# Row-tiled matmuls of 32 rows by 128 outputs issued as four of 32 by 32 in a cross network

## The chip, the cores and the metric

The kernel runs on one NeuronCore of a Trainium2 chip. The metric is the device time of one execution in microseconds (us); lower is better. The engines named below are TensorE (PE: matmuls; its weight loads are listed apart as PEld), VectorE (DVE), ScalarE (ACT), GpSimd (POOL) and SyncE (SP, which here issues most of the DMAs).

## The reference

A six-layer cross network (DCN v2) over a batch of 4096 rows with 416 features, all in bfloat16:

```python
B, F, D, L = 4096, 26, 16, 6
Din = min(F * D, 1024)          # 416
x0: (B, Din)   ws: (L, Din, Din)   bs: (L, Din)

def reference(x0, ws, bs):
    x = x0
    for l in range(ws.shape[0]):
        x = x0 * (x @ ws[l] + bs[l]) + x
    return x
```

## The kernel before

**Layout.** Through the first five layers the activations are held transposed: features on the 128 partitions, batch along the free dimension. 416 features are three full blocks of 128 (`XM`, indexed by k on the input side and m on the output side) and a remainder of 32. The batch is two halves (`s`) of 2048, and each half is four groups (`g`) of 512 columns. The remainder would fill only 32 partitions, so the remainders of the four groups are stacked: `XR` holds group g's 32 features on partitions 32g to 32g+31. The weight rows that belong to the remainder (`WR`) stand four times in SBUF, once on each of these strips, so that each group finds its weights on its own partitions.

**TensorE as tiles.** A matmul here has a tile position (row, column) in the 128 by 128 array, in steps of 32. Its rows are the partitions of the two inputs, its columns the partitions of the PSUM output. Matmuls at different positions can stand in the array at the same time. Three helpers issue the matmuls of layers two to five:

- `mm_full` (L181): for one output block m and one group g, the three k blocks, each as four matmuls of 128 rows and 32 outputs at the column positions 0, 32, 64, 96. The four write the four partition quarters of one PSUM bank.
- `mm_row` (L187): the share of the remainder in output block m, for all four groups at once: four matmuls of 32 rows and 128 outputs at the row positions 0, 32, 64, 96. Group g writes the whole of its own bank, `pts[g // 2][:, g % 2, :]`. This is the function that is changed.
- `mm_rem` (L193 and L198): the 32 outputs of the remainder, for all four groups, as matmuls of 128 rows and 32 outputs.

**PSUM.** Each output block of one half takes two PSUM tiles of two banks (`new_pts`); the pool holds four such tiles, which is all eight banks.

**Elementwise.** `ew_main` (L165, L166, L169) takes a PSUM tile of 128 by 1024: ScalarE adds the bias and writes bfloat16 to SBUF, VectorE multiplies by x0 and adds the old x. `ew_rem` (L173 to L175) does the same for the remainder.

**Order.** Layers two to five (l = 1 to 4) take the six pairs of half and output block two at a time, ta and tb. TensorE's order in one such step is: `mm_full` of ta for the four groups (48 matmuls), `mm_row` of ta, which closes ta's sums, `mm_row` of tb, which opens tb's sums, then `mm_full` of tb (48 matmuls), which closes them. So two `mm_row` calls stand next to each other, and a layer has three such row blocks, twelve over the four layers. After the first step of a layer `mm_rem` runs for both halves. The order in the program is the order on the engine; the tile framework puts semaphore waits where a buffer or an input demands it.

The first layer (`first_layer`: L214 full products of 128 by 128, L221 row products) and the last layer (L327, L333, L336: the activations become the stationary side so that rows of the batch come out on the partitions) have helpers of their own.

Of the kernel before, what the change touches and what calls it, by code (L numbers as in the profile page):

```python
# [16 lines left out]
def kernel(  # L17
# [7 lines left out]
    nc = tc.nc  # L25
# [7 lines left out]
    NG = 4  # L33
    CW = 512
# [18 lines left out]
    WR = const.tile([P, L, D], BF16)  # L53
# [129 lines left out]
                                 tile_position=(0, 32 * q))  # L183

    def mm_row(l, s, m, pts, curR, first, last):
        for g in range(NG):
            nc.tensor.matmul(pts[g // 2][:, g % 2, :], lhsT=WR[32 * g:32 * g + 32, l, 128 * m:128 * m + 128],  # L187
                             rhs=curR[32 * g:32 * g + 32, CW * s:CW * s + CW],
                             start=first, stop=last, tile_position=(32 * g, 0))

    def mm_rem(l, s, pr, cur, curR):
        for g in range(NG):
# [88 lines left out]
    cur, curR = XM[1], XR[1]  # L281
    for l in range(1, LL):
# [3 lines left out]
        pts = {}  # L286
# [8 lines left out]
        for n in range(0, len(tiles), 2):  # L295
            ta, tb = tiles[n], tiles[n + 1]
            pts[ta] = new_pts()
            for g in range(NG):
                mm_full(l, ta[0], ta[1], g, pts[ta], cur, True, False)
            mm_row(l, ta[0], ta[1], pts[ta], curR, False, True)  # L300
            pts[tb] = new_pts()
            mm_row(l, tb[0], tb[1], pts[tb], curR, True, False)
            if feeds_last and n == 4:
                xl_rem(0)
            finish(ta)
            for g in range(NG):
                mm_full(l, tb[0], tb[1], g, pts[tb], cur, False, True)
            finish(tb)
            if n == 0:
                rem_pair(l, cur, curR, nxtR, feeds_last)  # L310
        if feeds_last:
            xl_rem(1)
        cur, curR = nxt, nxtR

    l = LL
# [97 lines left out]
```

## Time and profile before

| what | before |
|---|---|
| time, median of 3 runs | 131.17 us (130.72 to 131.19) |
| span of the profiled execution, first to last instruction | 128.9 us |
| median less that span, what lies around it | 2.3 us |
| TensorE matmuls busy | 123.1 us, 96% of the span |
| VectorE busy | 107.1 us, 83% |
| ScalarE busy | 86.9 us, 67% |
| granted TensorE clock, mean | 0.998 of full speed |
| one layer of layers three to five (46.2 to 65.4, 65.4 to 84.6, 84.6 to 103.8 us) | 19.2 us each |
| L187, matmuls of 32 by 128 with 512 columns | 96, mean 379 ns each |
| L181, matmuls of 128 by 32 with 512 columns | 1152, mean 379 ns each |

How to read it: matmuls are pipelined and several stand in the array at once, so their lengths overlap and must not be added up; the end of a matmul is modelled. What counts is when the next one starts. In the views, `32*128 32x512 bf16 x8` means eight matmuls on 32 rows and 128 columns of the array that each stream 32 partitions by 512 elements. In the chain of work that ended last, each line is a start, a length, and the work that filled it. "idle before <-releaser" is the time in which the engine stood before the instruction, and what ended it; "issue" means that nothing in the profile explains the wait.

### The profile page before, as it was taken

To read this page: it belongs to the slowest core of one execution; us is meant where nothing else is said; L and a number is where in the kernel's file an instruction comes from. 1 tells how busy PE (TensorE), PEld (TensorE's weight loads), DVE (VectorE), ACT (ScalarE), POOL (GpSimd) and SP (SyncE) were. 2 spreads that over 40 slices of the span, in tenths; PEclk is the share of its full clock that TensorE was granted. 3 is DMA by queue.
4 is the path that set the end of the run, shared out by engine and by line. 5 is a ranking of instruction groups with operands and counts; after the bars stand their busy time and mean duration, and the time that the engine had idled before them with its cause. 6 is when DMAs were issued, how large, how long until landed. Compare 5 with 4: busy or idle time off the path is not lost.

```text
span 128.9 us, 3973 instructions
## 1 busy us (share of the span) xinstructions
PE 123.1 (96%) x1690; PEld 54.9 (43%) x1690; DVE 107.1 (83%) x197; ACT 86.9 (67%) x99; POOL 5.9 (5%) x18
## 2 busy tenths in 40 slices
PE   6999999999999999999999999999999999999960
PEld 2343443354444444444444444444444445445420
DVE  1032979999999898989898989898989899898991
ACT  0426783987848577848668848668847896569670
POOL 4022200600000000000000000000000000000000
PEclk9999999999999999999999999999999999999999
DMA  3999999999990000000000000000297999995754
GB/s 106 237 203 217 170 158 260 247 328 333 336 299 11 5 0 8 0 0 5 0 5 0 5 0 5 0 5 0 42 166 164 123 219 178 187 323 188 231 179 139
DMA packets 42102, 16.37 MB, mean 127 GB/s; under 512 B 30906, under 2 KB 42084, under 8 KB 42084
## 3 DMA queue, kind: packets, MB, share of 16 engines
q1 hardware_dynamic: 39416, 15.56, 54.6%
q10 hardware_dynamic: 2668, 0.56, 2.3%
q8 instruction: 13, 0.21, 0.7%
q14 instruction: 5, 0.04, 0.1%
HBM read 6.15 MB, written 3.41 MB: 74 GB/s over the span
## 4 chain that ended last, share of the span: by engine, by line
PE 80%; DMA 8%; DVE 5%; issue 2%; SPq 1%; ACT 1%; DVEq 0%
PE pt L181 49%; PE ph L214 9%; DMA XM<-in_x_dram 8%; PE py L327 8%; PE pt L187 5%; PE pr L198 5%; DVE t L355 3%; DVE o L344 2%; PE pr L193 2%; SPq L76 1%; PE py L333 1%; PE ph L221 1%; PE py L336 1%; ACT t L354 1%; PE pr L157 0%
## 5 line engine op out<-in xcount | busy, mean ns | idle before, releaser
L181 PE MATMUL pt<-XM,WM 128*32 128x512 bf16 x1152 | 65.2, 379 | 0.0
L165 ACT ACTIVATE t<-pt,bM 128x1024 bf16<-128x1024 f32 x48 | 49.6, 1115 | 18.3 <-PE pt L187 18.3
L166 DVE TENSOR_TENSOR t<-t,XM 128x1024 bf16<-128x1024 bf16 x60 | 41.4, 690 | 5.3 <-ACT t L165 5.3
L169 DVE TENSOR_TENSOR XM<-t,XM 128x1024 bf16<-128x1024 bf16 x60 | 41.8, 696 | 3.4
L181 PEld LDWEIGHTS <-WM 128*32 128x32 bf16 x1152 | 29.7, 97 | 33.8 <-issue 5.1
L354 ACT CAST t<-py 128x416 bf16<-128x416 f32 (+1 forms) x23 | 14.8, 642 | 4.8 <-PE py L327 2.1
L327 PE MATMUL py<-WM,XM 128*128 128x416 bf16 x96 | 17.7, 340 | 0.0
L214 PE MATMUL ph<-XM,WM 128*128 128x512 bf16 x72 | 16.5, 379 | 0.1
L165 ACT ACTIVATE t<-ph,bM 128x1024 bf16<-128x1024 f32 x12 | 12.5, 1114 | 4.4 <-PE ph L221 4.4
L327 PEld LDWEIGHTS <-XM 128*128 128x128 bf16 x96 | 9.0, 98 | 8.5 <-issue 1.4
L355 DVE TENSOR_TENSOR t<-t,X0rows 128x416 bf16<-128x416 bf16 (+1 forms) x23 | 10.4, 454 | 1.2 <-ACT t L354 1.2
L214 PEld LDWEIGHTS <-WM 128*128 128x128 bf16 x72 | 6.8, 98 | 8.6 <-issue 1.3
L344 DVE TENSOR_TENSOR o<-t,XLrows 128x416 bf16<-128x416 bf16 (+1 forms) x23 | 10.3, 451 | 0.0
L173 ACT ACTIVATE t<-pr,bR 128x512 bf16<-128x512 f32 x10 | 6.4, 684 | 2.7 <-PE pr L198 2.1
L198 PE MATMUL pr<-XM,WM 128*32 128x512 bf16 x120 | 8.2, 379 | 0.0
L187 PE MATMUL pt<-XR,WR 32*128 32x512 bf16 x96 | 7.3, 379 | 0.0
L141 PE MATMUL wps<-warm 128*128 128x512 bf16 (+1 forms) x11 | 4.4, 593 | 1.2 <-DVE warm L94 1.2
L175 DVE TENSOR_TENSOR XR<-t,XR 128x512 bf16<-128x512 bf16 x10 | 4.2, 423 | 0.7
L198 PEld LDWEIGHTS <-WM 128*32 128x32 bf16 x120 | 3.2, 97 | 3.1
L106 ACT ACT_TABLE_LOAD x1 | 1.3, 1283 | 4.3 <-DMA WM<-in_ws_dram 4.3
L174 DVE TENSOR_TENSOR t<-t,XR 128x512 bf16<-128x512 bf16 x10 | 4.2, 418 | 0.0
L152 DVE CAST bM<-pb 128x18 f32<-128x18 bf16 x1 | 0.2, 177 | 4.6 <-PE pb L151 4.6
(39 smaller groups left out, 33.6 us busy)
## 6 DMA issues: line engine op xcount, KB each, us to landing
X0rows<-in_x_dram SPq DMA_DIRECT2D x4, 832.0 KB, 11.6
out_dram<-o SPq DMA_DIRECT2D x9, 208.0 KB, 2.4
WM<-in_ws_dram SPq DMA_DIRECT2D x5, 312.0 KB
out_dram<-o SPq DMA_DIRECT2D x13, 104.0 KB, 1.7
WR<-in_ws_dram SPq DMA_DIRECT2D x4, 130.0 KB, 4.1
WM<-in_ws_dram ACTq DMA_DIRECT2D x1, 312.0 KB
XM<-in_x_dram SPq DMA_TRANSPOSE x8, 4.9
xrig<-in_x_dram ACTq DMA_DIRECT2D x4, 32.0 KB, 4.1
```

The source lines that it names most:

```text
L165: nc.scalar.activation(t[:], pt[:].rearrange("p a b -> p (a b)"), ACT.Identity, bias=bM[:, m, l:l + 1], scale=1.0)
L166: prod = nc.vector.tensor_tensor(out=t[:], in0=t[:], in1=XM[0][:, m, c0:c0 + 2 * CW], op=ALU.mult)
L169: nc.vector.tensor_tensor(out=nxt[:, m, c0:c0 + 2 * CW], in0=t[:], in1=cur[:, m, c0:c0 + 2 * CW], op=ALU.add)
L173: nc.scalar.activation(tr[:, 0:CW], pr, ACT.Identity, bias=bR[:, l:l + 1], scale=1.0)
L181: nc.tensor.matmul(pts[g // 2][32 * q:32 * q + 32, g % 2, :], lhsT=WM[:, l, k, 128 * m + 32 * q:128 * m + 32 * q + 32], rhs=cur[:, k, c0:c ...
L187: nc.tensor.matmul(pts[g // 2][:, g % 2, :], lhsT=WR[32 * g:32 * g + 32, l, 128 * m:128 * m + 128], rhs=curR[32 * g:32 * g + 32, CW * s:CW ...
L198: nc.tensor.matmul(pr[32 * g:32 * g + 32, :], lhsT=WM[:, l, k, NK * P:D], rhs=cur[:, k, c0:c0 + CW], start=False, stop=(k == NK - 1), tile ...
L214: nc.tensor.matmul(pt[:, gl, :], lhsT=WM[:, 0, k, 128 * m:128 * m + 128], rhs=cur[:, k, c0:c0 + CW], start=(k == 0 and not after_row), sto ...
L327: nc.tensor.matmul(py[:, 0:D], lhsT=cur[:, k, q_cols(q, g)], rhs=WM[:, l, k, :], start=((not closes) and k == 0), stop=(closes and k == NK ...
L344: tc.keep_in_program_order(nc.vector.tensor_tensor(out=o, in0=t, in1=xl, op=ALU.add))
L354: nc.scalar.copy(tv, src)
L355: tc.keep_in_program_order(nc.vector.tensor_tensor(out=tv, in0=tv, in1=X0rows[:, b, :], op=ALU.mult))
```

## The change

Only `mm_row` changes. Each matmul of 32 rows and 128 outputs becomes four of 32 rows and 32 outputs. Piece q reads the 32 weight columns of its outputs, writes the partitions 32q to 32q+31 of the same bank, and has the tile position (32g, 32q). The loop over q is outside, that over g inside, so four neighbouring matmuls have one column position and the four row positions. The inputs, the number of columns streamed (512), the start and stop flags and the calls around it stay. `mm_row` is called from layers two to five alone; the first layer has its own `row`.

```diff
     def mm_row(l, s, m, pts, curR, first, last):
-        for g in range(NG):
-            nc.tensor.matmul(pts[g // 2][:, g % 2, :], lhsT=WR[32 * g:32 * g + 32, l, 128 * m:128 * m + 128],
-                             rhs=curR[32 * g:32 * g + 32, CW * s:CW * s + CW],
-                             start=first, stop=last, tile_position=(32 * g, 0))
+        for q in range(4):
+            for g in range(NG):
+                nc.tensor.matmul(pts[g // 2][32 * q:32 * q + 32, g % 2, :],
+                                 lhsT=WR[32 * g:32 * g + 32, l, 128 * m + 32 * q:128 * m + 32 * q + 32],
+                                 rhs=curR[32 * g:32 * g + 32, CW * s:CW * s + CW],
+                                 start=first, stop=last, tile_position=(32 * g, 32 * q))
```

In the planned order each of the twelve row blocks has 64 instructions on TensorE where it had 16 (a weight load and a matmul each); all else on TensorE, and the whole order of the other four engines, is as before.

## The prediction

> **What bounds the kernel now.** I read the page first: the share of the engines, then the chain of work that ended last.
>
> ```profile
> PE 123.1 (96%) x1690; PEld 54.9 (43%) x1690; DVE 107.1 (83%) x197; ACT 86.9 (67%) x99; POOL 5.9 (5%) x18
> ...
> PE 80%; DMA 8%; DVE 5%; issue 2%; SPq 1%; ACT 1%; DVEq 0%
> PE pt L181 49%; PE ph L214 9%; DMA XM<-in_x_dram 8%; PE py L327 8%; PE pt L187 5%; PE pr L198 5%; DVE t L355 3%; DVE o L344 2%; PE pr L193 2%; SPq L76 1%; PE py L333 1%; PE ph L221 1%; PE py L336 1%; ACT t L354 1%; PE pr L157 0%
> ...
> L165 ACT ACTIVATE t<-pt,bM 128x1024 bf16<-128x1024 f32 x48 | 49.6, 1115 | 18.3 <-PE pt L187 18.3
> ...
> L187 PE MATMUL pt<-XR,WR 32*128 32x512 bf16 x96 | 7.3, 379 | 0.0
> ...
> q8 instruction: 13, 0.21, 0.7%
> ```
>
> The chain is 80% matmul, and the changed line L187 holds 5% of it. ScalarE waits 18.3 us in all for just that line, so what L187 gains or loses goes on to the engines behind it. Next the same chain in order of time, around the first changed block and at two older places:
>
> ```profile
> 16.20 0.65 PE pr L198 x12
> 16.85 0.33 PE pr L157 x4
> 17.18 3.88 PE ph L214 x18
> 21.06 0.54 PE ph L221 x8
> ...
> 26.90 2.59 PE pt L181 x48
> 29.49 0.54 PE pt L187 x8
> 30.03 2.71 PE pt L181 x48
> 32.74 0.21 PE pr L193 x4
> ```
>
> L181 runs four matmuls side by side in the four column strips of the array: 48 take 2.59 us, so a pass of four takes 2.59/12 = 0.216 us. L187 puts four side by side in the four row strips: 8 are two passes and should take 0.43, but take 0.54. The 48 of L181 behind them take 2.71 where 2.59 would do. So each change of tile shape costs about 0.11 us, and there are two for each of the 12 row blocks (96 matmuls, 8 in a block): 12 x 0.22 = 2.6 us in all. L181, L193 and L198 have one shape (128 rows, 32 columns), and no such step lies between them (0.21 for a pass). The two older places are changes of one dimension alone: from L198 (128 by 32) to L157 (128 by 128) four transposes of 128 columns, a quarter of 512, should take 4 x 0.216/4 = 0.22 us and take 0.33; from L214 (128 by 128) to L221 (32 by 128) two passes take 0.54 again. A change in one dimension is paid like one in both.
>
> Last the timeline of the same moment, on the matmul side and on the weight-load side, and one pass alone:
>
> ```profile
> 28.67 0.82 PE L181 MATMUL pt<-XM,WM 128*32 128x512 bf16 x12
> 29.42 0.61 PE L187 MATMUL pt<-XR,WR 32*128 32x512 bf16 x8
> 29.96 2.77 PE L181 MATMUL pt<-XM,WM 128*32 128x512 bf16 x48
> 32.56 0.39 PE L193 MATMUL pr<-XR,WD 128*32 128x512 bf16 x4
> ```
>
> ```profile
> 29.42 0.12 PEld L187 LDWEIGHTS <-WR 32*128 32x128 bf16 x8 [0.42 <-issue]
> 29.96 2.28 PEld L181 LDWEIGHTS <-WM 128*32 128x32 bf16 x48 [0.42 <-issue]
> ```
>
> Columns: start, length, engine, line, shape, count. Four matmuls with a modelled length of 0.379 to 0.381 cover 0.39 us, so three further starts fit in about 0.01 us: some 3.5 ns from one to the next. Eight loads of 92 ns cover 0.12, seven steps in 0.03: 4 ns, with four matmuls started between them. The idle 0.42 of the load side, charged to "issue", is the change of shape itself.
>
> **The change part by part.** The planned order of instructions on the other four engines is unchanged, and so is the place of each row block on TensorE. A block holds 16 instructions before (8 loads, 8 matmuls) and 64 after.
>
> 1. *Work per pass.* Before, a pass has four matmuls in four tiles of 32 by 128. After, it has 16 in 16 tiles of 32 by 32, each still streaming 512 columns. Each tile has its own place in the array and its own quarter of a PSUM bank: row strip g still writes bank g, column strip q only partitions 32q to 32q+31. If all 16 run together, the pass stays 0.216 us. No row shows 16 together. What bounds it: both halves are shown (four row strips together in L187, four column strips in L181, both 0.216), which gives +0; wholly one column strip after the other gives three passes more (rival C). I take +0, since the pattern is the product of two that are both seen to work.
>
> 2. *More starts.* 12 more matmuls, with their loads, start before the last one of the pass. At 3.5 ns each the last of 16 starts 15 x 3.5 = 53 ns after the first, against 10 ns now: +42 ns. The second pass follows tile by tile in the same stagger and does not pay it again; the change of shape behind it waits for the last start and does. So +42 ns per block, 12 x 42 = **+0.50 us**. This lies on the chain with nothing to hide it. Bounds of the spacing: nothing (the starts hidden behind the streaming) gives 0; the sustained rate of L181, 8 instructions in 216 ns or 27 ns each, gives 64 x 27 = 1.73 us per block against the 0.54 + 0.11 = 0.65 now, 12 x 1.08 = +13 us. Between these I take 3.5 ns, because L181's 27 ns is set by the streaming and not by issue, while the bursts of L187 and L193 show what issue alone does.
>
> 3. *Changes of shape.* 128 by 32 to 32 by 32 and back is still two changes per block, now in the rows alone. By the L214 to L221 row it costs the same 0.11: +0. If it cost nothing, -2.6 us (rival D).
>
> 4. *Counted at nothing.* 288 more matmuls and 288 more loads (96 to 384 each) make the program of TensorE longer: 0.21 MB for some 3,400 instructions is 62 bytes each, 36 KB more, two or three further instruction packets, and in these layers the DMA row of the page stands at 0. Were a packet late, TensorE would stand for that time. The results reach ScalarE 0.04 us later per block; its 18.3 us of waiting at 12 blocks is 1.5 each, so no PSUM buffer comes free too late (without that cover each 0.04 would be paid once more). VectorE is busy 83% of the time and catches up with ScalarE in every slice, so it shifts along with its input. No wait, DMA or queue is added.
>
> Sum: span 128.9 + 0.5 = 129.4. The median of the runs lies 131.17 - 128.9 = 2.3 us above the profiled span, which I leave as it is: **131.7 us**, +0.4%.
>
> **The rivals.**
>
> *B, the supply of instructions cannot follow a block of 64 (slower).* For: TensorE must take 64 instructions in about 0.65 us, 10 ns each, where over a whole 96-matmul stretch it now takes 27; no stretch of the trace shows such a rate for longer than a few dozen. Against: before each block the queue has had microseconds at 27 ns to run ahead. It decides once the spacing exceeds 10 ns and the lead is used up. At 16 ns without a lead, 64 x 16 = 1.02 instead of 0.65, 12 x 0.37 = +4.5; with a lead of half a block half of it is left, +2.2. I put B at +1 to +4.5, middle **133.5**. The Trainium skill, "TensorE: Matmul & The Clock Gate", Part 1, states a start-to-start floor of about 25 ns for small matmuls; as a rule for every start a pass of 16 would take 0.40 us, 12 x 2 x 0.18 = +4.4. The trace speaks against it between different tiles: four starts in 0.01 us.
>
> *C, tiles that share a row strip do not overlap (much slower).* Then q = 0 to 3 run one after another: 12 blocks x 2 passes x 3 x 0.216 = +15.6, **146.7**. Against it: L181's four tiles share all 128 rows, and their loads (48 in 2.28 us) run under the matmuls (48 in 2.77 us, both from 29.96). For it: 32-row tiles in one row strip have not been seen together. The Trainium skill, same page, Part 3, "The mechanism", has this as a rule: a weight load overlaps matmuls in flight only where the row group differs. By that rule alone the result would be C's; this trace's L181 contradicts it at least for 128-row tiles.
>
> *D, the change of shape gets cheaper (faster).* Only the row tiling changes now and the columns stay as they were; should the array not have to empty, 2.6 us go and the stagger of 0.5 stays: 131.17 - 2.1 = **129.1**. Against it: both one-dimension changes above are paid in full.
>
> That the split is not carried out is excluded: each block stands with its 64 instructions in the planned order.
>
> **How the numbers follow.** Likeliest case 0.50, B 0.28, C 0.08, D 0.14. About 0.5% (0.66 us) is what a measurement of this kernel can tell from no change; its three runs spread over 0.47 us. The likeliest case's own range is 131.2 to 132.3 (spacing of 0 to about 8 ns, and the spread); some two thirds of it count as no change, a third as slower. Slower: 0.17 + 0.28 + 0.08 = 0.53; same 0.33; faster 0.14. The range of 130.2 to 135.0 holds the likeliest case, nearly all of B and a partial D, and leaves out C and the full D.
>
> **What would show it.** Right: the 16 matmuls of a pass starting within 0.05 to 0.06 us, the chain's row block of 32 at 0.54 to 0.60 us, 0.11 more on the L181 stretch behind it, 0.42 of "issue" idle on the load side before and after. B: L187's successors spread with gaps inside a block, a block of 0.7 us or more, or a slow L181 stretch behind it. C: a block of 1.7 us and more. D: the idle 0.42 gone and 2.59 for the 48 of L181 behind the block. My prediction is wrong if the 32 take under 0.45 or over 0.65 us.

## The result and the profile after

Over 20 runs of each kernel the median goes from 130.97 to 131.34 us. The ratio is 1.0038, 95% interval 1.0026 to 1.0050, which is 0.34 to 0.65 us slower. The forecast was 131.7 us against the 131.17 shown then, a ratio of 1.004. The sum made in the trace comes out at +0.45 us, as shown below.

The page of the changed kernel, lines as shown of the kernel before:

```profile
PE 123.0 (95%) x1976; PEld 56.0 (43%) x1978; DVE 107.3 (83%) x197; ACT 86.8 (67%) x99; POOL 6.0 (5%) x18
...
q8 instruction: 15, 0.25, 0.7%
...
PE 80%; DMA 8%; DVE 5%; issue 2%; SPq 1%; ACT 1%; DVEq 0%
...
L165 ACT ACTIVATE t<-pt,bM 128x1024 bf16<-128x1024 f32 x48 | 49.5, 1116 | 19.1 <-PE pt L188 19.1
...
L188 PE MATMUL pt<-XR,WR 32*32 32x512 bf16 x384 | 7.8, 379 | 0.0
...
L188 PEld LDWEIGHTS <-WR 32*32 32x32 bf16 x384 | 2.4, 87 | 5.1 <-issue 5.1
```

L188 is the changed line. It has four times the matmuls (384), and the time they cover goes from 7.3 to 7.8 us. ScalarE waits 0.8 us longer for them. Two more packets of instructions are loaded. The last line still has 5.1 us of unexplained idle time in front of the row blocks, as the same loads had before:

```profile
L187 PEld LDWEIGHTS <-WR 32*128 32x128 bf16 x96 | 1.4, 92 | 5.1 <-issue 5.1
```

So the change of tile shape is still paid.

The chain of work that ended last, in order of time, around the first row block:

```profile
27.16 2.59 PE pt L181 x48
29.75 0.58 PE pt L188 x32
30.33 2.70 PE pt L181 x48
33.03 0.22 PE pr L195 x4
```

The block takes 0.58 us where it took 0.54. The L181 stretch in front takes 2.59 and the one behind 2.70, as before. So the whole change sits in the block. In the timeline (start, length, engine, line, shape, count), matmuls and then loads:

```profile
29.68 0.65 PE L188 MATMUL pt<-XR,WR 32*32 32x512 bf16 x32
30.26 2.77 PE L181 MATMUL pt<-XM,WM 128*32 128x512 bf16 x48
```

```profile
29.68 0.20 PEld L188 LDWEIGHTS <-WR 32*32 32x32 bf16 x32 [0.42 <-issue]
30.25 2.28 PEld L181 LDWEIGHTS <-WM 128*32 128x32 bf16 x48 [0.38 <-issue]
```

32 loads of 87 ns cover only 0.20 us, and 32 matmuls with a modelled length of 379 ns cover 0.65: all 16 tiles are in flight together. Taken from the start times of the single instructions in the trace, the same in all twelve blocks within 1 or 2 ns:

| ns | before (4 tiles) | after (16 tiles) |
|---|---|---|
| last L181 matmul to first row matmul | 312 | 309 |
| first to last start of a pass | 10 | 50 |
| first start of pass one to first start of pass two | 226 | 226 |
| last row matmul to first L181 matmul behind | 304 | 304 |
| in all, last L181 matmul in front to first behind | 852 | 889 |

The difference is 37 ns, and 12 x 37 = 0.45 us. The stretch from the first to the last L181 start goes from 76.74 to 77.19 us, +0.45: nothing else in it has moved. The profiled span grew by 0.70. The other 0.25 us lies in front of that stretch (its first start comes at 26.98 instead of 26.73, behind the first loads of x0), in lines that the change does not touch. What lies behind it is equal: 20.74 us to the last matmul against 20.73.

### The profile page after: what moved, and what is told of

It is laid out like the page before. It is cut to its first block, busy times and chain, and to the rows that moved or that the text cites. A ratio compares the mean times of both kernels' runs of the same rounds, so it can differ in the third digit from the quotient of the medians.

```text
span 129.6 us, 4547 instructions
## 1 busy us (share of the span) xinstructions
PE 123.0 (95%) x1976; PEld 56.0 (43%) x1978; DVE 107.3 (83%) x197; ACT 86.8 (67%) x99; POOL 6.0 (5%) x18
## 4 chain that ended last, share of the span: by engine, by line
PE 80%; DMA 8%; DVE 5%; issue 2%; SPq 1%; ACT 1%; DVEq 0%
PE pt L181 49%; PE ph L216 9%; DMA XM<-in_x_dram 8%; PE py L329 8%; PE pt L188 5%; PE pr L200 5%; DVE t L357 3%; DVE o L346 2%; PE pr L195 2%; SPq L76 1%; PE py L335 1%; PE ph L223 1%; PE py L338 1%; ACT t L356 1%; PE pr L157 0%
## 5 line engine op out<-in xcount | busy, mean ns | idle before, releaser
L181 PE MATMUL pt<-XM,WM 128*32 128x512 bf16 x1152 | 65.2, 379 | 0.0
L181 PEld LDWEIGHTS <-WM 128*32 128x32 bf16 x1152 | 29.8, 97 | 33.3 <-issue 4.6
L188 PE MATMUL pt<-XR,WR 32*32 32x512 bf16 x384 | 7.8, 379 | 0.0
L141 PE MATMUL wps<-warm 128*128 128x512 bf16 (+1 forms) x11 | 3.9, 534 | 1.2 <-DVE warm L94 1.2
L188 PEld LDWEIGHTS <-WR 32*32 32x32 bf16 x384 | 2.4, 87 | 5.1 <-issue 5.1
```

Of the source, the lines that this page charges most:

```text
L181: nc.tensor.matmul(pts[g // 2][32 * q:32 * q + 32, g % 2, :], lhsT=WM[:, l, k, 128 * m + 32 * q:128 * m + 32 * q + 32], rhs=cur[:, k, c0:c ...
L188: nc.tensor.matmul(pts[g // 2][32 * q:32 * q + 32, g % 2, :], lhsT=WR[32 * g:32 * g + 32, l, 128 * m + 32 * q:128 * m + 32 * q + 32], rhs= ...
```

## The experiments

Every variant below computes the same result. "Block" is the last line of the table above, from the trace; "stretch" is the time from the first to the last start of the full products of layers two to five.

**Does the order of the pieces matter?** `e1_g_outer` swaps the two loops of the changed kernel:

```diff
-        for q in range(4):
-            for g in range(NG):
+        for g in range(NG):
+            for q in range(4):
```

> Loop order swapped in mm_row: the four column pieces of one row strip are now neighbours. Theory S (the cost is the extra starts, about 3.3 ns each, that the next change of shape waits for): nothing depends on the order, so the first start of a row block to the last again spans 226 + 50 ns, a block is 0.58 us on the chain and the span stays within 0.3 us of the changed kernel. Rival R (tiles that share a row strip get in each other's way, and the order with the row strips inside hid it): loads wait for matmuls of their strip, the starts of a pass spread well over 50 ns, and the block grows to 0.65 us or more, +0.8 us or more in all.

```profile
29.54 0.58 PE pt L188 x32
30.12 2.70 PE pt L181 x48
```

These are lines of its chain. The starts of a pass again spread over 50 ns, the block is 889 ns and the stretch 77.19 us; all three are equal to the changed kernel's. The single run took 131.19 us beside 130.73 for the kernel before. Tiles that share a row strip do not get in each other's way, in either order. Rival R falls, and rival C of the prediction with it.

**Does the price follow the number of starts?** `e2_two_of_64` splits each product in two:

```diff
-        for q in range(4):
+        for q in range(2):
...
-                nc.tensor.matmul(pts[g // 2][32 * q:32 * q + 32, g % 2, :],
-                                 lhsT=WR[32 * g:32 * g + 32, l, 128 * m + 32 * q:128 * m + 32 * q + 32],
+                nc.tensor.matmul(pts[g // 2][64 * q:64 * q + 64, g % 2, :],
+                                 lhsT=WR[32 * g:32 * g + 32, l, 128 * m + 64 * q:128 * m + 64 * q + 64],
...
-                                 start=first, stop=last, tile_position=(32 * g, 32 * q))
+                                 start=first, stop=last, tile_position=(32 * g, 64 * q))
```

> Two pieces of 64 outputs in place of four of 32: 8 starts in a pass instead of 4 or 16. Theory S: seven steps of 3.3 ns, 23 ns, so from the last L181 matmul before a block to the first behind it about 862 ns, between 852 (4 starts) and 889 (16 starts), +0.13 us in all over the kernel before. Rival P (the price goes with the narrow tiles or the changed pair of shapes, not with the number of starts): 852 or 889 and nothing between.

The lines of the diff are against the changed kernel. The stagger is as expected: 23 to 24 ns from the first to the last of eight starts, between 10 and 50. The block is 877 ns, between 852 and 889, so rival P falls, but it is 15 ns more than expected. The trace puts that in one place. From pass one to pass two it takes 240 ns where both other shapes take 226; the entry (last L181 matmul to first row matmul, 309) and the exit (last row matmul to the first L181 matmul behind, 304) are those of the changed kernel. So the first pass behind a change of shape takes 24 ns beyond the 216 of a steady pass with weights 64 columns wide, and 10 ns with 32 or 128. That wait goes with the weights' shape, and was in no theory. The loads themselves are longer with 64 columns, 103 ns against 87 and 92:

```profile
L188 PEld LDWEIGHTS <-WR 32*64 32x64 bf16 x192 | 1.9, 103 | 5.1 <-issue 5.1
```

I read it as a wait for the weights; no run shows that it is. The stretch is 77.04 us, +0.30 = 12 x 0.025. The single run of 132.65 us is not a measure of it: its last output transfer landed 2.59 us after VectorE's last instruction, where the other profiles have 1.4.

**Is a change of one dimension cheaper?** In `e5_full_128` the row products are as before the change, and the full products have 128 columns, so going into a row block changes the rows alone (lines against the kernel before):

```diff
         for k in range(NK):
-            for q in range(4):
-                nc.tensor.matmul(pts[g // 2][32 * q:32 * q + 32, g % 2, :], lhsT=WM[:, l, k, 128 * m + 32 * q:128 * m + 32 * q + 32],
-                                 rhs=cur[:, k, c0:c0 + CW], start=(first and k == 0), stop=(last and k == NK - 1),
-                                 tile_position=(0, 32 * q))
+            nc.tensor.matmul(pts[g // 2][:, g % 2, :], lhsT=WM[:, l, k, 128 * m:128 * m + 128],
+                             rhs=cur[:, k, c0:c0 + CW], start=(first and k == 0), stop=(last and k == NK - 1))
```

> mm_row as before the change (32 by 128), but mm_full as one matmul of 128 by 128 per k block instead of four of 128 by 32, so entering and leaving a row block changes the rows alone, as the row split meant it with the columns alone kept. Theory S (every change of either dimension is paid in full): the block stays at 0.85 us from matmul to matmul, and mm_rem (128 by 32) now needs two changes of its own in each layer: 8 x 0.10 = +0.8 us less up to 0.2 for slightly shorter passes, so +0.5 to +0.9 us over the kernel before. Rival D (a change of one dimension is cheaper): the block falls below 0.80 us and the time is at or under that of the kernel before.

```profile
29.69 0.54 PE pt L185 x8
30.23 2.70 PE pt L180 x12
32.93 0.33 PE pr L191 x4
33.26 0.65 PE pr L196 x12
33.91 0.22 PE pr L191 x4
34.12 0.65 PE pr L196 x12
34.77 2.70 PE pt L180 x12
```

The chain: the row block (L185) takes 0.54 as in the kernel before, and 854 ns in the trace. The remainder product (L191, 128 by 32) now costs 0.33 where it follows another shape and 0.22 where it follows its own, and the stretch behind it 2.70 instead of 2.59. The ratio is 1.0062 (1.0038 to 1.0085), +0.5 to +1.1 us; the stretch grows by 0.78. Each change costs its 0.1 us, whichever dimension changes.

**What does a third change inside the block cost?** In `e6_mixed` the closing call uses 16 tiles, the opening one four:

```diff
     def mm_row(l, s, m, pts, curR, first, last):
+        if not first:
             for q in range(4):
                 for g in range(NG):
...
+            return
+        for g in range(NG):
+            nc.tensor.matmul(pts[g // 2][:, g % 2, :], lhsT=WR[32 * g:32 * g + 32, l, 128 * m:128 * m + 128],
...
+                             start=first, stop=last, tile_position=(32 * g, 0))
```

> The closing mm_row call (first pass of a block) in 16 tiles of 32 by 32, the opening one (second pass) in four of 32 by 128, so a third change of shape, of the columns alone, lies inside each block. Theory S: 309 + 50 + 304 + 10 + 304 = 977 ns from the last L181 matmul before a block to the first behind it, against 852 before and 889 for the changed kernel: 12 x 0.125 = +1.5 us over the kernel before. Rival D (a change of columns among row-tiled shapes is free): about 860 to 890 ns and no more than +0.5 us.

```profile
29.16 0.36 PE pt L189 x16
29.52 0.33 PE pt L195 x4
29.85 2.70 PE pt L181 x48
```

Two passes take 0.36 + 0.33 = 0.69 us on the chain, where the changed kernel takes 0.58. The block is 1001 ns, 24 more than expected: 317 at the inner change and 314 at the exit, where 304 was expected for each. Each of the two row shapes has one pass only here, and I read 10 ns of either as the longer first pass. The stretch grows by 1.79 us = 12 x 0.149. The ratio is 1.0176 (1.0159 to 1.0193), +2.1 to +2.5 us, which is 0.3 or more above the stretch of its one profile. The profiled execution, 132.17 us, is the shortest of the five; the others took 132.87 to 133.10, and where they spent the rest is not known. D's rule for columns alone falls too.

**Is the supply of instructions near its limit?** `e3_cols_256` and `e4_cols_128` keep the 16 tiles and stream each product in two or four parts, so that a block holds 128 or 256 instructions instead of 64:

```diff
+        W = CW // 2
+        for c in range(2):
             for q in range(4):
                 for g in range(NG):
-                nc.tensor.matmul(pts[g // 2][32 * q:32 * q + 32, g % 2, :],
+                    nc.tensor.matmul(pts[g // 2][32 * q:32 * q + 32, g % 2, W * c:W * c + W],
...
-                                 rhs=curR[32 * g:32 * g + 32, CW * s:CW * s + CW],
+                                     rhs=curR[32 * g:32 * g + 32, CW * s + W * c:CW * s + W * c + W],
-                                 start=first, stop=last, tile_position=(32 * g, 32 * q))
+                                     start=(first and c == 0), stop=(last and c == 1), tile_position=(32 * g, 32 * q))
```

These are lines of `e3_cols_256` against the changed kernel, with the lines that stay as they are indented there; in `e4_cols_128` both 2s are 4, and `c == 1` is `c == 3`.

> The 16 tiles of 32 by 32, each product streamed as two matmuls of 256 columns: 128 instructions in a row block instead of 64, in the same time. Theory S with a supply that is not the limit: a pass of 256 columns is 108 ns, longer than the 53 ns in which 16 tiles start, so the block stays at 309 + 10 + 3 x 109 + 50 + 197 = about 0.89 us from matmul to matmul, and the span at the changed kernel's within 0.3 us. Rival B (the supply of instructions limits once its lead of some 44 is used up): gaps inside the block; at 10 ns an instruction 128 take 1.28 us and the kernel +4 to +7 us.

> Each product streamed as four matmuls of 128 columns: 256 instructions in a row block. A pass of 128 columns is 55 ns, about as long as the 16 tiles take to start. Theory S without a supply limit: eight passes of 55 to 60 ns, about 0.90 us from matmul to matmul, span within 0.5 us of the changed kernel. Rival B: at 10 ns an instruction 2.6 us a block, +20 us in all; the spacing of the starts once the lead is used up is the rate of the supply itself.

The two took 136.08 and 150.7 us, one run each, beside 130.91 for the kernel before. Chain of `e3_cols_256`, around its second row block:

```profile
35.03 2.67 PE pt L181 x48
37.70 0.81 PE pt L190 x64
38.51 1.19 PE pt L181 x20
39.70 1.64 issue
41.34 4.29 PE pt L181 x76
45.62 0.81 PE pt L190 x64
```

and of `e4_cols_128`, its first block and its third:

```profile
30.18 1.25 PE pt L190 x128
31.43 1.19 PE pt L181 x20
32.63 2.94 issue
35.57 1.69 PE pt L181 x28
...
49.78 1.25 PE pt L190 x128
```

There are two costs here. The first is the block: 0.81 and 1.25 us instead of 0.58, though the columns streamed are the same. From matmul to matmul it is 1118 and 1557 ns, where theory S expected about 890 and 900, and rival B 10 ns an instruction; neither was met. The starts in a block of `e3_cols_256`, in ns from its first matmul, are

```
0, 3, 6, 10, ... 50 | 120, 122, 126, ... 170 | 305, 313, 321, 330, ... 538, 572, 581, 615
```

The first 32 matmuls, 64 instructions with their loads, start 3.3 ns apart within a pass, as in the changed kernel. Then nothing starts for 135 ns, and from there on one matmul starts every 8.3 ns. `e4_cols_128` does the same: 32 matmuls within 116 ns, none for 136 ns, then one every 8.3 ns. The count does not hang on the passes: where TensorE stood inside a block of `e4_cols_128`, behind 20 matmuls of the second block and 84 of the fourth, again 32 started in a burst, then none for 118 to 119 ns, then one every 8.3 ns. So about 64 instructions stand ready when TensorE starts again, and I read the 8.3 ns a pair as the rate at which further ones come. The Trainium skill, "TensorE: Matmul & The Clock Gate", in the table at its head, gives TensorE a queue of 64 instructions; these traces agree, with 64 started before the gap. Rival B names a real mechanism, and the changed kernel's block of exactly 64 stops just short of it. No run has a block between 64 and 128.

The second cost is the piece marked "issue": TensorE stands. In `e3_cols_256` it stands once, 1.64 us, with 957 weight loads and matmuls started. In `e4_cols_128` it stands five times: 2.94 us at 701 started, 0.24 at 957, 1.12 at 1213, 0.32 at 1981 and 3.28 at 5821. All these counts are 701 plus a multiple of 256, and an instruction packet is 16 KB or, at some 62 bytes each, about 260 instructions. In all six stops the packet that had started last did so 2.3 to 2.6 us before TensorE went on. In `e3_cols_256` it started at 38.71 us and took 1.09; TensorE went on at 41.34, 2.63 us after the start. The DMA share in the view of stretches is 1.10 from 38.0 to 38.7 us and 0.22 from there to 39.8. I read this as code that arrives late, in `e3_cols_256` because the input loads fill the DMA queues until the packet starts. Full queues are not needed for it: from the packet's start to the end of the stops of 1.12 and 0.32 us the DMA share is 0.00 and 0.03. No run was made to part late code from other causes. In the changed kernel the packet of that place started at 38.90, and the 958th of these instructions started at 42.20 without a stop. Were it to need the same 2.63 us, it would have come 0.7 us in time.

The +5.2 us of `e3_cols_256` lies in rival B's +4 to +7, but of the 5.1 us in its stretch the blocks hold 12 x 0.266 = 3.2 and TensorE's standing most of the rest, which B did not count. Rival B's +20 us for `e4_cols_128` is met by luck alone: of the 19.3 us that its stretch grows over the kernel before, the twelve blocks without their stops hold 12 x 0.705 = 8.5 us, and most of the rest is the stops.

## Why the prediction was right

*What bounds the kernel.* TensorE is still 80% of the chain, and the 0.45 us added to its stretch arrive at the end in full: from the last matmul to VectorE's last instruction it is 2.12 us in both profiles.

*Step 1, the pass.* Taken at +0, and it is: 226 ns from pass to pass with 4 and with 16 tiles. The product of two patterns that had each been seen held, in both loop orders.

*Step 2, more starts.* Predicted 53 ns less 10, +42 a block and +0.50 us. Measured 50 less 10, and 3 off at the entry, where the first matmul follows its own load instead of two: +37 a block, +0.45 us. `e2_two_of_64` with eight starts shows the same slope, 3.3 ns a start. The upper bound of 27 ns an instruction was far off: once the queue is empty, `e3_cols_256` shows 8.3 ns for a pair.

*Step 3, changes of shape.* Taken at +0. The exit stayed at 304 ns, and `e5_full_128` and `e6_mixed` show the price for rows alone and for columns alone. What I did not set apart is the longer first pass (10 ns, or 24 with 64 columns): the prediction's 0.11 of a change holds it, and it is the same before and after the change. The sum for `e2_two_of_64` took 10 for 64 columns too, and the one for `e6_mixed` left the 10 ns out at the inner change and the exit; that is most of why they were too low.

*Step 4, counted at nothing.* Two more packets (13 to 15), and no stop in the L181 stretches. "The DMA row stands at 0" was misread: it holds for the middle of these layers, but the DMA share of the kernel before is 1.08 from 26.9 to 38.7 us, where the first two row blocks lie, and 0.96 from 97.0 to 103.8. The cover at the end of the input loads was thin, by the packet of `e3_cols_256` an estimated 0.7 us, and the prediction had no number for it.

*The rivals.* C is refuted by the table and by `e1_g_outer`, D by `e5_full_128` and `e6_mixed`. B did not happen: 16 matmuls start in 50 ns and the pass takes 226, not the 0.40 us that was weighed for it. But its point of decision was put in the wrong terms. I took a rate of 10 ns an instruction and a lead of half a block, and for `e3_cols_256` a lead of some 44, which no run shows; what decides in these runs is whether a block fits in about 64 instructions. With twice as many the block loses 0.23 us, 12 x 0.23 = 2.7 us, and the kernel another 1.8 us at the one stop.

*The rule on row groups.* The Trainium skill, "TensorE: Matmul & The Clock Gate", Part 3, "The mechanism", which the prediction weighed for C, has weight loads overlap matmuls in flight only across row groups. Here 32 loads in four row strips cover 0.20 us under matmuls of the same strips, so these traces disagree with it for loads to other column tiles.

## What to carry to other kernels

Splitting a row-tiled matmul into narrower column tiles does not buy time where the four row tiles already fill the array: the pass stays as it is, every extra start adds 3.3 ns to the end of the block, and the next change of tile shape waits for it. Count changes of tile shape rather than which dimension changes; each costs about 0.1 us here. Before multiplying instructions, ask whether a burst fits in the about 64 that started here without a gap, and whether the code for it is loaded in time.

## What the runs showed of the hardware that was not expected

The first pass behind a change of shape takes 10 ns more than a steady one with weights of 32 or 128 columns, and 24 ns more with 64.

A burst on TensorE runs at 3.3 ns a matmul and load for about 64 instructions; past that, nothing starts for about 0.12 to 0.14 us, and then a pair every 8.3 ns.

In the stop of 3.28 us in `e4_cols_128` (116.27 to 119.54 us) the granted clock fell to half, at 119.04, and stayed there for about 3.4 us. The stop of 2.94 us in the same run left it at 1.00. The view of stretches shows the fall, with the clock in the column before the DMA share:

```profile
112.00:116.00 4.00, 4.00 (x166) 2.25 (x159) 3.55 (x6) 2.14 (x4) 0.00 (x0) 1.00 1.07 127
116.00:119.00 3.00, 0.27 (x26) 0.14 (x17) 1.98 (x3) 1.94 (x2) 0.00 (x0) 1.00 1.06 122
119.00:122.50 3.50, 2.96 (x40) 1.21 (x43) 0.69 (x1) 0.00 (x0) 0.00 (x0) 0.51 1.03 154
```
